# Rearranging the opening of a Fourier-mixing and MLP kernel: x ahead of the weights, exponents on GpSimd, weight conversion between the first steps

## The chip, the cores and the metric

The kernel runs on one core of one Trainium2 chip. The metric is the device time of one execution in microseconds (us), as the median of several; most times of one kernel agree within about 0.3%, and a difference counts as faster or slower only beyond 2%. The profile is one execution recorded by the hardware profiler. Its engines are PE (TensorE's matmuls), PEld (its weight loads), DVE (VectorE), ACT (ScalarE), POOL (GpSimd) and SP (SyncE, which here only issues DMAs).

## The reference, cut to what matters

```python
x:     (8, 3008, 256) float32
w_in:  (256, 2048), w_out: (2048, 256)      # reach the kernel as float64

X = np.fft.fft(np.fft.fft(x, axis=1), axis=2).real     # mixing, then 24064 tokens
h = X @ w_in
g = h * np.clip(h + 3.0, 0.0, 6.0) / 6.0               # hard swish
return g @ w_out
```

## The kernel before

The sequence transform is split as 3008 = 47 x 64. *Stage 1* transforms over 47 (after VectorE has folded x by its symmetry), the result z goes through a scratch buffer zd in DRAM, comes back as g, and *stage 2* transforms over 64 into q; a small `spread` makes the row qn. The 256-wide transform is folded into w_in. Two batches form a pair; a pair has 12 chunks of tokens, a chunk 8 steps over the hidden dimension. One step is two products u and v (`mlp1`), s, relu and gates on VectorE and ScalarE, and seven half-size block products (`mlp2`, in place of eight, paid for with sums that GpSimd makes in `combine`).

The float64 weights come as 16 pieces of 0.5 MB and are turned to float32 on the chip. Per piece:

```python
def exponent_a(j):            # ScalarE, twice: top bits to two numbers, PM
    nc.scalar.activation(low, top, AF.Identity, bias=..., scale=...)
def exponent_b(j):            # TensorE: their difference, into PSUM
    for i in range(2):
        nc.tensor.matmul(ex[:], E[:, i], PM[:, j % 2, i].bitcast(F16), ...)
def exponent_c(j):            # ScalarE: to the bits of a power of two
    nc.scalar.activation(exs[j][:].bitcast(I32), exs[j][:], AF.Identity, scale=2.0 ** 23)
def mantissa(j):              # VectorE, two operations ("top")
    ...
def join(j):                  # VectorE: mantissa times power ("wi", or blocks of G)
    ...
```

Pieces of w_in are then multiplied by the transform on TensorE (the *fold*, `wps`); pieces of w_out are mixed into seven blocks of G. The schedule is by hand: the order in which the program issues an engine's instructions is the order in which the traces show them. In the opening the pieces travel beside x; 15 of the 16 are read before the first step, and the last is finished beside the first few (its join ran at 100.18 us):

```python
for c in range(NXC):                    # 8 chunks of x
    if c + 2 < NXC:
        load_x(first, c + 2)
    load_w(c + 2)
    fold_first(first, c)                # (the last chunk: fold)
    on_scalar(c); on_vector(c)          # one step of the conversion pipeline
    ...stage 1...
    on_tensor(c)
load_g(first, 0)
for j in range(NXC, 15):                # the other pieces
    load_w(j + 2); on_scalar(j); on_vector(j); keep_awake(1); on_tensor(j)
...
for i in range(2):
    stage2(first, 0, i)
spread(first, 0)
...
for s, (p, ck, fc) in enumerate(steps): # 384 steps
    mlp1(*chunk(s + 2)); combine(*chunk(s + 1)); ...; mlp2(*chunk(s))
```

Of the kernel before, what the change touches and what calls it, by code (L numbers as in the profile page):

```python
# [51 lines left out]

PROD = ("P1", "P2", "-P4", "P5", "P7", "-P6", "P3")
# [3 lines left out]
def kernel(  # L57
# [51 lines left out]
    F = consts.tile([PR + 2, 5 * PZ + NP * NXC + 1], F32, name="F")  # L109
# [17 lines left out]
    def x_tile(pr, i):  # L127
        pool, tag = xpool, "x"
        if pr.p == 0 and 4 <= i < 13:
            pool, tag = ((apool, "a"), (cpool, "c"), (spool, "t"))[(i >= 8) + (i >= 11)]  # L130
        return pool.tile([PR + 2, XC, D], F32, tag=tag, name="xt")
# [8 lines left out]
    def load_forward(pr, c):  # L140
        xt = x_tile(pr, 2 * c)

        nr = PR + 2 if pr.p < NP - 1 else PR
        rows = x_pn[pr.p * PR:pr.p * PR + nr]
        n = XC if c < NXC - 1 else XC - 1
        nc.gpsimd.dma_start(out=xt[0:nr, 0:n, :], in_=rows[:, c * XC + 1:c * XC + 1 + n, :])
        if n < XC:
            nc.gpsimd.dma_start(out=xt[0:nr, n:XC, :], in_=rows[:, 0:1, :])
        pr.x[c] = xt

    def load_partners(pr, c):
        xr = x_tile(pr, 2 * c + 1)
# [31 lines left out]
    def fold_first(pr, c):  # L184
        xt, xr = pr.x[c][0:PR], pr.xr[c][0:PR]
        r = xr[:, ::-1, :]
        y = ypool.tile([PR, XC + 1, D], F32, tag="y", name="y")
        tt = nc.vector.tensor_tensor
        tt(y[:, 0:XC, 1:P], xt[:, :, D - 1:P:-1], r[:, :, 1:P], op=AL.add)
        tt(xt[:, :, 1:P], xt[:, :, 1:P], r[:, :, D - 1:P:-1], op=AL.add)  # L190
        tt(xt[:, :, 0:P + 1:P], xt[:, :, 0:P + 1:P], r[:, :, 0:P + 1:P], op=AL.add)
        pr.y[c] = y

    def stage1_first(pr, c, i):
        sl = slice(2 * i, 2 * i + 2)
        a, b = pr.x[c][0:PR, sl, :], pr.y[c][:, sl, 1:P]
        ps = bank([P, 2, D], "ps1")
        for k, (f, m, c0) in enumerate([(F[0:PR, 0:PZ], a[:, :, 0:P + 1], 0), (F[0:PR, 0:PZ], b, 1),
                                        (F[0:PR, 0:PZ], a[:, :, 1:P], P + 1), (FN[0:PR], b, P + 1)]):
            nc.tensor.matmul(ps[0:PZ, :, c0:c0 + m.shape[2]], f, m, start=(k == 0), stop=(k > 0),  # L200
                             skip_group_check=True)
        evict_z(pr, c, i, ps)
        if i == XC // 2 - 1:
            del pr.x[c], pr.xr[c]
# [9 lines left out]
    def stage1(pr, c, i):  # L214

        y = pr.y[c]
        ps = bank([P, 2, D], "ps1")
# [10 lines left out]
        evict_z(pr, c, i, ps)  # L228

    def evict_z(pr, c, i, ps):  # L230
        if i == 0:

            pool, tag = (gpool, "g") if pr.p == 0 and c % 3 == 2 else (zpool, "z")
            pr.z[c] = pool.tile([PZ, XC, D], F32, tag=tag, name="z")
            if c == 0:
                pr.zd = dpool.tile([2, NK1, 2, NS, D], F32, tag="zd", name="zd")
                pr.zq = dpool.tile([2, NK1, 2, NS], F32, tag="zq", name="zq")
        z = pr.z[c]
        nc.scalar.copy(z[:, 2 * i:2 * i + 2, :], ps[0:PZ])  # L239
        if i == XC // 2 - 1:  # L240
            nc.sync.dma_start(
                out=pr.zd[:].rearrange("b k c n d -> (b k c) n d")[:, c * XC:(c + 1) * XC, :],
                in_=z[:],
            )
            turn_column(pr, c, z)
            del pr.y[c], pr.z[c]
# [4 lines left out]
    def turn_column(pr, c, z):  # L251
        n = XC if c < NXC - 1 else XC - 1
        zc = zpool.tile([PZ, XC], F32, tag="zc", bufs=4, name="zc")
        nc.scalar.activation(zc[:, 0:n], z[:, 0:n, P], AF.Identity, scale=F[0:PZ, 5 * PZ + NP * NXC:])
        cs = slice(c * XC, c * XC + n)
        nc.sync.dma_start(out=pr.zq[:, :, ::-1, cs].rearrange("b k c n -> (b k) c n"), in_=zc[:, 0:n])
        if n < XC:
            nc.sync.dma_start(out=pr.zq[:, :, :, c * XC + n].rearrange("b k c -> (b k c)"), in_=z[:, n, P])


    def load_g(pr, gr):
        g = gpool.tile([P, 2 * KK, D + 1], F32, tag="g", name="g")
        ks = slice(gr * 2 * KK, (gr + 1) * 2 * KK)
        gb = [g[b * N2:(b + 1) * N2] for b in range(2)]
        for b in range(2):
            nc.sync.dma_start(out=gb[b][:, :, 0:D], in_=pr.zd[b].rearrange("k c n d -> (c n) k d")[:, ks, :])
        for b in range(2):
            nc.sync.dma_start(out=gb[b][:, :, D], in_=pr.zq[b].rearrange("k c n -> (c n) k")[:, ks])
# [36 lines left out]
    class Chunk:  # L305
# [3 lines left out]
        def __init__(self, pr, ck):  # L309
            self.pr, self.ck = pr, ck  # L310
            self.last = ck == NCK - 1
            self.final = self.last and pr.p == NP - 1
# [81 lines left out]

    def mlp2(ch, fc):
# [78 lines left out]
    FN = wpool.tile([PR + 2, PZ], F32, tag="FN", name="FN")  # L474
# [8 lines left out]
    raw, exs, fracs, w = {}, {}, {}, {}  # L483

    def load_w(j):
        kind, n, i = PIECES[j]
        st = wpool.tile([P, 2 * WB], I32, tag="st", bufs=4, name="st")
# [17 lines left out]
    def exponent_a(j):  # L505
        top = raw[j][:].bitcast(I16).rearrange("p (n four) -> p n four", four=4)[:, :, 3]
        for i in range(2):
            low = PM[:, j % 2, i].bitcast(U8).rearrange("p (n two) -> p n two", two=2)[:, :, 0]
            nc.scalar.activation(low, top, AF.Identity, bias=bias[:, i:i + 1], scale=(1 - 2 * i) / 16.0)  # L509

    def exponent_b(j):
        ex = ps_h.tile([P, WB], F32, tag="uv", name="ex")
        for i in range(2):
            nc.tensor.matmul(ex[:], E[:, i], PM[:, j % 2, i].bitcast(F16), start=(i == 0), stop=(i == 1))  # L514
        exs[j] = ex
# [4 lines left out]
    def mantissa(j):  # L520
# [3 lines left out]
        top = wpool.tile([P, WB], I32, tag="top", bufs=2, name="top")  # L524
# [5 lines left out]
    def join(j):  # L530
        kind, n, i = PIECES[j]
        frac, ex = fracs.pop(j), exs.pop(j)[:]
        if kind == "in":
            o = wpool.tile([P, WB], F32, tag="wi", bufs=4, name="wi")
            nc.vector.tensor_tensor(o[:], frac, ex, op=AL.mult)
# [3 lines left out]
        b12 = wpool.tile([P, 2, P], F32, tag="b12", bufs=2, name="b12")[:] if i == 0 else None  # L539
        for h, g in enumerate((block(n, 0), b12) if i == 0 else (block(n, 1), block(n, 6))):  # L540
            f, e = (t.rearrange("p (c q h e) -> h p c q e", c=2, h=2, e=DH)[h] for t in (frac, ex))
            nc.vector.tensor_tensor(g.rearrange("p c (q e) -> p c q e", e=DH), f, e, op=AL.mult)
        if i == 0:
            w[PIECES[j]] = b12
# [4 lines left out]
    def use_pair(j):  # L549
        kind, n, _ = PIECES[2 * j]  # L550
        if kind == "in":
            fold_w_in(n)
        else:
            mix_w_out(n)

    def mix_w_out(j):

        b12 = w.pop(("out", j, 0))
        g = [block(j, i) for i in range(7)]
        tt = nc.vector.tensor_tensor  # L560
        tt(g[3], g[0], b12, op=AL.subtract)
        tt(g[5], g[6], g[3], op=AL.add)
        tt(g[2], g[5], g[1], op=AL.subtract)
        tt(g[4], g[6], b12, op=AL.subtract)

    def fold_w_in(n):

        cs = slice(n * WB, (n + 1) * WB)
        ws = [w.pop(("in", n, i)) for i in range(2)]
        sums = []  # L570
        for blk in range(2):
            ps = bank([P, WB], "wps")
            for i in range(2):
                nc.tensor.matmul(ps[:], C[:, i, blk * P:(blk + 1) * P], ws[i], start=(i == 0), stop=(i == 1))  # L574
            sums.append(ps)

        def copy():
            for blk in range(2):
                nc.scalar.copy(W1[:, blk, cs], sums[blk][:])
            nc.sync.dma_start(out=wn[n:n + 1], in_=W1[P - 1:P, 1, cs])  # L580

        copies.append(copy)


    def load_wn(n):
        nb = WB // P
        nc.sync.dma_start(out=WN[:, n * nb:(n + 1) * nb], in_=wn[n].rearrange("(j p) -> p j", p=P))
# [263 lines left out]
```

## Time and profile before

| | before |
|---|---|
| time, median of 3 | 1980.33 us (1979.98 to 1984.44) |
| span of the profiled run, mean clock granted to TensorE | 1978.3 us, 0.996 |
| TensorE busy | 1949.1 us, 99% |
| first u; end of the eighth step's products | 80.06 us; 132.4 us |

The page of the profile gives busy times and the chain of work that ended last; windows give busy time per engine in a stretch; the order in time gives start, duration, engine, source line, operation, output and inputs, and in brackets how long the engine sat idle before and what ended that. The lines of before are in the prediction.

### The profile page before, as it was taken

The page shows a single profiled execution, that of the slowest core. Times are in us where ns is not written, and L with a number is a line of the kernel's source. Part 1 is how long each engine was busy: PE and PEld are TensorE (multiplying, and loading weights), DVE is VectorE, ACT ScalarE, POOL GpSimd, SP SyncE. Part 2 cuts the span into 40 slices and gives each one's busy share as a digit, 9 for nine tenths or more (in the row PEclk, how much of TensorE's full clock was granted, in tenths as well). Part 3 has the DMA queues.
Part 4 walks back from the last instruction along what each step waited for, and adds up shares of the span by engine and source line. Part 5 has one row for each costly group of instructions (what it writes and reads, how often), then busy time and mean ns, then how long its engine had stood idle before and what let it go on. Part 6 is the DMA issues. An engine that isn't in the chain of part 4 may idle for free.

```text
span 1978.3 us, 27746 instructions
## 1 busy us (share of the span) xinstructions
PE 1949.1 (99%) x9178; PEld 1685.4 (85%) x9178; DVE 1433.5 (72%) x2775; ACT 687.9 (35%) x1164; POOL 1414.2 (71%) x1604
## 2 busy tenths in 40 slices
PE   8899999999999999999999999999999999999998
PEld 5588888888998888888898888888889888888887
DVE  5677767776787776776777776777678777777776
ACT  6533333333333333333333333333333333333332
POOL 4277778786687787777768877778667667666765
PEclk9999999999999999999999999999999999999999
DMA  9502211111111111221111221212110101111000
GB/s 307 136 26 61 51 41 46 49 49 35 27 36 51 41 49 48 54 59 24 36 32 30 63 55 44 56 41 54 37 22 23 30 14 25 26 24 28 17 20 20
DMA packets 149701, 93.31 MB, mean 47 GB/s; under 512 B 121739, under 2 KB 135055, under 8 KB 149558
## 3 DMA queue, kind: packets, MB, share of 16 engines
q1 hardware_dynamic: 139294, 57.86, 12.2%
q0 software_dynamic: 9472, 33.49, 5.9%
q8 instruction: 72, 1.18, 0.2%
q14 instruction: 71, 0.58, 0.1%
q10 hardware_dynamic: 792, 0.20, 0.0%
HBM read 54.19 MB, written 37.33 MB: 46 GB/s over the span
## 4 chain that ended last, share of the span: by engine, by line
PE 93%; DVE 2%; ACT 1%; issue 0%; DMA 0%; SPq 0%; DVEq 0%; ACTq 0%
PE acc L403 56%; PE v L334 16%; PE u L334 16%; PE ps L284 2%; PE ps L227 2%; DVE a L379 1%; DVE s L339 1%; ACT t L376 0%; ACT PM L509 0%; DVE o L461 0%; PE wps L574 0%; DVE u L360 0%; PE ps L224 0%; PE ex L514 0%; PE awake L597 0%
## 5 line engine op out<-in xcount | busy, mean ns | idle before, releaser
L393 POOL TENSOR_TENSOR c<-a 128x512 f32<-128x512 f32 (+1 forms) x383 | 478.2, 1248 | 431.4 <-PE acc L403 369.3
L403 PE MATMUL acc<-c,G 128*128 128x256 f32 (+1 forms) x3072 | 712.0, 375 | 0.0
L376 ACT ACTIVATE t<-u,half 128x512 f32<-128x512 f32 (+1 forms) x384 | 261.0, 680 | 1100.5 <-DVE u L349 1018.7
L403 PEld LDWEIGHTS acc<-c,G 128*128 128x128 f32 x3072 | 577.5, 190 | 72.7
L339 DVE SCALAR_TENSOR_TENSOR s<-qn,WN,u 128x256 f32<-128x256 f32 (+1 forms) x768 | 330.0, 471 | 354.3 <-PE u L334 354.0
L403 PE MATMUL acc<-a,G 128*128 128x256 f32 (+1 forms) x2304 | 551.2, 375 | 0.0
L403 PEld LDWEIGHTS acc<-a,G 128*128 128x128 f32 x2304 | 433.8, 190 | 55.9
L334 PE MATMUL v<-q,W 127*128 127x256 f32 (+1 forms) x1536 | 390.1, 376 | 4.4 <-DVE a L379 4.4
L334 PE MATMUL u<-q,W 128*128 128x256 f32 (+1 forms) x1536 | 388.3, 375 | 2.4 <-DVE a L379 2.1
L379 DVE SCALAR_TENSOR_TENSOR a<-t,u 128x512 f32<-128x512 f32 (+2 forms) x448 | 263.7, 600 | 104.9 <-ACT t L376 102.1
L334 PEld LDWEIGHTS u<-q,W 128*128 128x128 f32 x1536 | 285.7, 190 | 58.2 <-issue 14.8
L334 PEld LDWEIGHTS v<-q,W 127*128 127x128 f32 x1536 | 288.7, 190 | 45.1 <-DVE a L379 4.1
L393 POOL TENSOR_TENSOR c<-c,a 128x256 f32<-128x256 f32 (+1 forms) x383 | 274.8, 717 | 30.0
L393 POOL TENSOR_TENSOR c<-a,c 128x256 f32<-128x256 f32 (+1 forms) x383 | 274.6, 717 | 30.1
L349 DVE TENSOR_TENSOR u<-s,v 128x512 f32<-128x512 f32 x352 | 245.0, 696 | 37.7 <-PE v L334 0.8
L379 DVE SCALAR_TENSOR_TENSOR a<-t,v 128x512 f32<-128x512 f32 (+1 forms) x480 | 263.2, 564 | 0.0
L376 ACT ACTIVATE t<-v,half 128x512 f32<-128x512 f32 (+1 forms) x384 | 260.5, 678 | 0.0
L351 DVE TENSOR_TENSOR v<-v,s 128x512 f32<-128x512 f32 x352 | 243.7, 692 | 0.0
L393 POOL TENSOR_TENSOR r<-w,e 128x256 f32<-128x256 f32 (+1 forms) x94 | 90.8, 987 | 3.7
L411 ACT ACTIVATE e<-acc 128x512 f32<-128x512 f32 (+2 forms) x190 | 86.3, 545 | 3.4 <-PE acc L403 3.3
L461 DVE STREAM_TRANSPOSE o<-r 128x256 f32<-128x256 f32 (+1 forms) x192 | 72.5, 414 | 0.2
L239 ACT COPY z<-ps 96x512 f32<-96x512 f32 x64 | 37.2, 582 | 83.7 <-PE ps L227 65.2
(91 smaller groups left out, 780.2 us busy)
## 6 DMA issues: line engine op xcount, KB each, us to landing
out_dram<-o SPq DMA_DIRECT2D x746, 32.0 KB
zd<-z SPq DMA_DIRECT2D x32, 384.0 KB
g<-zd SPq DMA_DIRECT2D x48, 256.0 KB
xt<-in_x_dram POOLq DMA_DIRECT2D x21, 384.0 KB, 4.1
qn<-qd SPq DMA_DIRECT2D x19, 256.0 KB
st<-in_moe_w_in_dram POOLq DMA_DIRECT2D x8, 512.0 KB, 9.1
st<-in_moe_w_out_dram POOLq DMA_DIRECT2D x8, 512.0 KB, 5.1
xt<-in_x_dram POOLq DMA_DIRECT2D x7, 376.0 KB, 3.9
```

Of the source, the lines that this page charges most:

```text
L227: nc.tensor.matmul(ps[0:PZ], F[0:PR, 0:PZ], y[:, 2 * i:2 * i + 2, :], start=True, stop=True)
L284: nc.tensor.matmul(ps[:, blk, u * P:n].rearrange("p (b k) -> p b k", b=2), g[:, kk, blk * (P + 1):blk * (P + 1) + P], T[:, :, gr, blk, kk, ...
L334: nc.tensor.matmul(ps[:, i, 0:nq], W1[r, blk, f * P:(f + 1) * P], q[r, blk, of:of + nq], start=True, stop=True)
L339: nc.vector.scalar_tensor_tensor(s[:, i, 0:nq], qn[:, of:of + nq], WN[:, f:f + 1], u[:, i, 0:nq], op0=AL.mult, op1=AL.add)
L349: nc.vector.tensor_tensor(u[:], s[:], v[:], op=AL.add)
L351: nc.vector.tensor_tensor(v[:], v[:], s[:], op=AL.subtract)
L376: nc.scalar.activation(t, h, AF.Relu, bias=half[:], scale=scale)
L379: nc.vector.scalar_tensor_tensor(dst, t, 1.0, h, op0=AL.min, op1=AL.mult)
L393: (eng or nc.gpsimd).tensor_tensor(out, in0, in1, op=AL.add)
L403: nc.tensor.matmul(ch.acc[i // 2][:, i % 2, 0:ch.n], G[:, i, fc, :], mv, start=(fc == 0 and i % 2 == 0), stop=(fc == NF - 1), skip_group_c ...
L411: nc.scalar.mul(ch.e[:, k:i + 1, 0:ch.n], ch.acc[i // 2][:, 0:i + 1 - k, 0:ch.n], 1.0 / WS)
L461: nc.vector.transpose(o[:, 0:n // DH, h], ch.r[:, m, h, 0:n].rearrange("p (j i) -> p j i", i=DH))
```

## The change

The intent: TensorE is the bound, and only in the first 132 us does it do other work than the result's. So x is loaded ahead of all weights; only the 16 of 96 scratch rows of z that the first group of tokens needs are stored at once, the others later; GpSimd subtracts the exponents in place of TensorE; the fold of w_in is made in halves of 256 columns; only pieces 0 to 5 are converted before the first step, the others between the first eight steps; and the first chunk is done by eight plain block products (as four of 512 columns), which need no mixed G. Cut to its core:

```diff
 def exponent_a(j):
     ...
-def exponent_b(j):
-    ex = ps_h.tile([P, WB], F32, tag="uv", name="ex")
-    for i in range(2):
-        nc.tensor.matmul(ex[:], E[:, i], PM[:, j % 2, i].bitcast(F16), ...)
+    nc.gpsimd.tensor_tensor(exs[j][:], *(PM[j % 2][:, i].bitcast(F16) for i in range(2)), op=AL.subtract)
 def join(j):
-            nc.vector.tensor_tensor(o[:], frac, ex, op=AL.mult)
+            (nc.vector if starting[0] else nc.gpsimd).tensor_tensor(o[:], frac, ex, op=AL.mult)
...
+                nc.sync.dma_start(out=zd[0:n0], in_=z[0:n0])       # first group
+                later.append((zd[n0:], z[n0:]))
+            pool, tag = (zpool, "z") if k < 2 else (apool, "a") if k < 6 else (qpool, "q")   # where z lies
...
+def mlp2_first(ch, fc):                       # plain products, no combine
+    for h in range(2):
+        for f in range(2):
+            nc.tensor.matmul(ch.acc[h][:], G[:, (B11, B12, B21, B22)[2 * f + h], fc, :], a[:, :, f], ...)
...
+def head(j):
+    exponent_a(j); mantissa(j)
+    if j in NEXT: load_w(NEXT[j])
+def tail(j):
+    exponent_c(j); join(j)
+    ...                                       # notes the folds that are due
...
+for c in ORDER[0:3]:
+    load_x(first, c)
+for k, c in enumerate(ORDER):
+    ...fold, stage 1, load_x of chunk k + 3; pieces only when x is through...
+load_g(first, 0)
+head(0); head(1); keep_awake(1); tail(0); keep_awake(1, w[PIECES[0]])
+head(2); tail(1); fold_w_in(*folds.pop(0)); head(3); tail(2); copy_all(); tail(3); head(4)
+for i in range(2): stage2(first, 0, i)
+spread(first, 0)
+fold_w_in(*folds.pop(1)); copy_all()
+for dst, src in later: nc.sync.dma_start(out=dst, in_=src)
...
+DUE = [(6, 7), (8, 9, 10), (11, 12), (13, 14), (15,), (), (), ()]
+mlp1(*chunk(0)); ...folds...; tail(4); head(5); tail(5)
 for s, (p, ck, fc) in enumerate(steps):
+    if s < NF:
+        for j in DUE[s][:1]: head(j)
+        copy_all()
+        mlp1(*chunk(s + 1))
+        for j in DUE[s][:1]: tail(j)
+        for j in DUE[s][1:2]: head(j)
+        mlp2_first(*chunk(s))
+        for j in DUE[s][1:2]: tail(j)
+        for j in DUE[s][2:]: head(j)
+        fold_all()
+        for j in DUE[s][2:]: tail(j)
+        ...
```

## The prediction

> **What bounds the kernel now.** I read the page from the top: busy shares, slices, the chain that ended last, then the first 140 us by tens and in order of time.
>
> ```profile
> PE 1949.1 (99%) x9178; PEld 1685.4 (85%) x9178; DVE 1433.5 (72%) x2775; ACT 687.9 (35%) x1164; POOL 1414.2 (71%) x1604
> ...
> PE 93%; DVE 2%; ACT 1%; issue 0%; DMA 0%; SPq 0%; DVEq 0%; ACTq 0%
> ```
>
> TensorE (PE) is the bound for the whole span, so nothing but its own work counts, except in the opening. There PE's busy time holds much that isn't the result: warming, waits, weight conversion. The chain, in order of time, shows where the dense part begins:
>
> ```profile
> 92.06 3.53 PE acc L403 x14
> ...
> 108.31 1.13 PE v L334 x4
> 109.44 3.02 PE acc L403 x14
> 112.46 0.86 PE u L334 x4
> 113.33 0.86 PE v L334 x4
> ...
> 129.34 3.02 PE acc L403 x14
> ```
>
> One step is u 0.86, v 0.86, seven products 3.02: 4.74 us, and there are 384 (4 pairs, 12 chunks, 8 steps). From 108 us on they are back to back. The eighth step's products end at 129.34 + 3.02 = 132.4 us, with ten steps' u and v done and both halves of the second group's stage 2. That is my marker: behind it 1846 us follow (1978.3 - 132.4), which the change hardly touches. The case is what happens to 132.4.
>
> ```profile
> 40.00:50.00 10.00, 7.02 (x29) 4.29 (x28) 7.90 (x22) 6.63 (x12) 0.74 (x2) 0.93 1.04 355
> 50.00:60.00 10.00, 9.72 (x26) 5.27 (x25) 5.95 (x10) 5.69 (x10) 2.15 (x3) 0.73 0.60 163
> 60.00:70.00 10.00, 8.86 (x23) 3.52 (x22) 4.28 (x9) 6.69 (x12) 1.42 (x2) 1.00 0.85 221
> 70.00:80.00 10.00, 8.15 (x38) 4.79 (x38) 7.69 (x19) 5.65 (x10) 0.00 (x0) 1.00 0.66 147
> ```
>
> The columns after each stretch are PE, PEld, DVE, ACT and POOL busy, clock, DMA share, GB/s. Up to 50 us the DMA engines are full (286 to 355 GB/s): x of the first pair (8 chunks of 0.77 MB, estimated from shapes) shares them with weight pieces of 0.5 MB. From 50 to 77 us it is one weight piece after another, in order:
>
> ```profile
> 69.28 1.40 ACT L509 ACTIVATE PM<-st,bias 128x512 uint8<-128x512 int16 x2
> 71.15 0.58 ACT L518 ACTIVATE ex<-ex 128x512 int32<-128x512 f32 x1 [0.46 <-PE ex L514]
> 71.64 1.40 ACT L509 ACTIVATE PM<-st,bias 128x512 uint8<-128x512 int16 x2
> 73.50 0.58 ACT L518 ACTIVATE ex<-ex 128x512 int32<-128x512 f32 x1 [0.46 <-PE ex L514]
> ```
>
> Each costs ScalarE 1.40 + 0.58 plus a wait for PE: 2.36 us. Stage 2 (77.4) and the first u (80.06) stand behind them.
>
> [...]four VectorE 128x256 ops took 0.42 us at 70 us, GpSimd idle, and 1.11, 0.83, 0.83, 1.48 at 101 us beside GpSimd adds. [...]here 717 ns against 0.42 us for 128x256, and 1248 ns against 0.69 for 128x512. [...]the trace grants 0.73 in 50 to 60 us, after gaps[...]. [...]last store issued at 55.35, load that waits for it at 57.40[...].
>
> **The change part by part.**
>
> *x first.* Three chunks are in flight; chunk k+3 is issued when chunk k is folded. Indices now arrive by a small load of their own, so the first fold starts at about 8.4 (9.11 before). A full fold on VectorE is four ops 0.61 apart and a small one, 2.6 us (first chunk 2.9, as the last one took before). Loading takes some 1.8 us of issue plus 4.5 to landing (median 5.1 for the gather, 4.1 at best): 6.2. So three chunks take 2.6 + 6.2 = 8.8, and the last fold ends near 8.4 + 2.9 + 2 x 8.8 + 2.6 = 31.5. PE needs only two products of 0.86 and a small one per chunk; stage 1 ends at 33.3 (before 53.7), the last copy of z at 33.9. The first group's stores (1/6 of the bytes) land by 37.5 beside weight loads, its g at 42.
>
> *Conversion.* GpSimd subtracts the two halves (128x512, 1.25 us) in place of two PE products. Per piece: ScalarE 1.41, GpSimd 1.25, ScalarE 0.58, join. Pieces 0 to 3 in ScalarE's order from 33.9: second weight block joined at 40.1, PE's half fold (1024 columns, 1.72) ends at 41.8. Stage 2 and spread, 2.7 us, run from 42.0; second half fold 44.7 to 46.4; copy 47.0; first u at 47.0 (80.06 before: 33 us earlier). [...]the first s is at 49.7 and gates end at 53.3.
>
> *What comes back.* Eleven pieces now lie between the first eight steps, each on the in-order queues of ScalarE and GpSimd. PE work from 47.0 to the marker: ten u and v, 17.2; eight plain block products (four of 512 columns, 2048 for 1792: 3.45 us each) 27.6; six half folds 10.3; stage 2 halves 1.8. Sum 56.9, end 103.9 with no wait. But piece 5 starts only after the first step's relu: 53.2 ScalarE, GpSimd subtraction to 57.0 (one VectorE op in between[...]), 57.6, G written by 59.5; first products end at 60.5, PE idle from 53.6. Pieces 6 and 7 follow; PE's folds of them wait until 66.8 and end at 70.2. Step 2: u, v, products to 75.4; folds of pieces 8 and 9 wait for 79.2, end 82.6. Step 3 needs piece 11's G: ends at 89.3. Then PE runs nearly free: 94.5, 99.7, 104.9, 110.1, 116.2, and 118.7 with the last u and v and the stage 2 halves. Waits thus 14.8 us of the 71.7.
>
> Gain: 132.4 - 118.7 = 13.7 us. Of the 33 us won at the first u, 14.8 go to new waits and about 5 to PE work moved behind it: folds 10.3 and plain products 3.4 more, less the 8 or so that PE lost between steps before. Time: 1980.3 - 13.7 = 1966.6; I put 1966.
>
> **The rivals.** *PE-bound opening:* conversion hides under PE. For it: ScalarE needs in steps 1 to 5 some 10 pieces x 2.0 + 6.9 of relu + 3.5 of copies = 30 us, PE 33. Against: both queues are in order and alternate through GpSimd. It would give 104 at the marker, 1952. [...]If each of 22 ops waits 0.6 us more than I placed, and half reaches PE, 6 to 7 us are lost: 1973. *The x pipeline:* if loads land in 7 to 8 us, as before under load (up to 15), stage 1 ends 3 to 5 us later: 1970. *A wait in the steady part:* the second group's spread is now at step 12, needed at 14, with 16 stores of results ahead of it in SyncE's queue at about 0.6 us each. 9.5 us of slack[...]: a few us at most. *Nothing gained:* every us won at the first u returns as waits, 1978. I doubt it; before, PE spent 27 us on conversion alone.
>
> **Range and chances.** Terms add, and each is uncertain by 3 to 6 us; hops of semaphores[...] are left out, and so is a cold clock, while overlap of issues goes the other way. 1952 to 1978. Faster by 2% is below 1940.7: it needs the marker at 92.8, below the 103.9 without any wait, hence 0.03. Slower by 2% (2020) would need damage in the steady part: 0.02.
>
> **What would show it.** Right: last stage 1 product near 33, first u near 47, first products ending near 60, PE busy under 70% between 50 and 85 us with waits put to GpSimd (wi and G), eighth products ending near 116, and the steady part equal within 2 us. Wrong: first u after 52 (x pipeline or g slower), no PE gap before the folds (PE-bound), the last G after 105, GpSimd ops of 128x512 f16 well over 1.3 us, or PE waits after step 10.

The 717 and 1248 ns are GpSimd's adds of 128x256 and 128x512 in the trace of before (`c`), the 0.42 and 0.69 us beside them VectorE's operations of these shapes.

## The result

The changed kernel took 1988.60 us (median of 4, 1986.19 to 1991.45) where the kernel before took 1980.15 in the same rounds: 8.45 us more. The ratio is 1.0038, with a 95% interval of 1.0019 to 1.0057. Ratios here are the mean time of one kernel's fast runs over that of the other's of the same rounds, so not quite the ratio of the medians. The verdict at 2% is "same", but the time is outside the predicted range.

The page of the changed kernel, busy times and the chain by engine:

```profile
PE 1942.8 (98%) x9074; PEld 1670.4 (84%) x9074; DVE 1439.6 (72%) x2754; ACT 686.5 (35%) x1162; POOL 1434.3 (72%) x1627
...
PE 92%; DVE 3%; DMA 2%; ACT 1%; issue 1%; POOL 1%; SPq 0%; DVEq 0%; ACTq 0%; POOLq 0%
```

PE does 6.3 us less work, and yet the end comes 8.7 us later (spans 1987.0 and 1978.3): it waits more. DMA, which had 0% of the chain, now has 2%. From its longest pieces in order of time (start, us, what), and its last steps before the steady part:

```profile
36.38 5.22 DMA zd<-z
...
42.41 6.75 DMA g<-zd
...
49.30 3.59 PE ps L285 x16
...
58.42 4.93 DMA zd<-z
...
75.94 5.23 PE spare L583 x14
...
91.24 6.10 PE spare L583 x14
...
102.67 4.42 PE acc L405 x6
...
131.36 3.44 PE acc L405 x8
...
138.93 1.13 PE v L336 x4
```

The store of z, the load of g, a store that the first gates wait for, and then PE groups that take 3.59, 5.23, 6.10 and 4.42 us, where the same groups at full clock, in runs told below, take 2.02, 3.29, 3.29 and 2.84. The eighth step's products end at 131.36 + 3.44 = 134.8 us (before: 132.4; predicted: 116.2). The 1.13 of v at the end follows a wait of 1.54 us for a gate, at the place where the program goes over from one step ahead to two.

The same windows as those that the prediction shows of before, and one more (columns after each stretch: PE, PEld, DVE, ACT and POOL busy, granted clock, DMA share, GB/s):

```profile
40.00:50.00 10.00, 5.48 (x13) 3.25 (x14) 7.43 (x9) 5.28 (x10) 3.86 (x4) 0.62 0.73 240
50.00:60.00 10.00, 9.76 (x51) 8.70 (x50) 3.00 (x6) 3.20 (x6) 2.12 (x2) 0.87 0.37 99
60.00:70.00 10.00, 6.41 (x22) 3.61 (x20) 6.25 (x13) 7.07 (x13) 6.40 (x8) 1.00 0.87 260
70.00:80.00 10.00, 5.26 (x14) 3.58 (x13) 4.54 (x5) 4.15 (x7) 6.35 (x7) 0.66 0.59 162
...
90.00:100.00 10.00, 8.69 (x24) 6.47 (x24) 4.93 (x6) 3.38 (x7) 4.94 (x5) 0.66 0.20 53
```

The columns to look at are PE busy and the clock. From 60 to 80 us PE is busy 11.7 of 20 us, and no other engine is full either: that is a chain of waits through all of them, not a bound. And in four of the five windows the clock is below 0.9, so that even the busy time is partly half speed (the granted clock was 0.50 from 44 to 52 us, for one). What such a chain looks like, in order of time, for pieces 8 and 9:

```profile
85.02 0.62 ACT L536 ACTIVATE ex<-ex 128x512 int32<-128x512 f32 x1
...
85.73 1.27 POOL L554 TENSOR_TENSOR wi<-top,ex 128x512 f32<-128x512 f32 x1 [8.06 <-ACT ex L536]
85.76 1.53 DVE L544 TENSOR_SCALAR top<-st 128x512 int32<-128x512 int32 x1
...
87.09 1.21 POOL L533 TENSOR_TENSOR ex<-PM 128x512 f32<-128x512 f16 x1
87.32 1.52 DVE L545 SCALAR_TENSOR_TENSOR top<-st,top 128x512 f32<-128x512 uint32 x1
...
89.14 0.74 POOL L515 DMA_DIRECT2D st<-in_moe_w_out_dram  x1 [0.85 <-DVE top L545]
...
89.91 1.28 POOL L554 TENSOR_TENSOR wi<-top,ex 128x512 f32<-128x512 f32 x1
...
91.24 6.10 PE L583 MATMUL spare<-wi,C 128*128 128x256 f32 x14 [3.49 <-POOL wi L554]
```

ScalarE's exponent of piece 8 comes only at 85.02 because it stands behind the relu of the step, which waits for PE's u and v (81.0). GpSimd had been idle for 8.06 us. Then GpSimd does join, subtraction, issue of the next load, join, one after the other; VectorE's mantissa operations, 0.42 and 0.69 us when GpSimd is idle, take 1.53 and 1.52 beside it; the issue of the load waits 0.85 us for the mantissa; and the folds on PE wait 3.49 us for the second join, and then run at half clock.

### The profile page after: what moved, and what is told of

Its sections match the earlier page's. It is cut to its first block, busy times and chain, and to the rows that moved or that the text cites. A ratio compares the mean times of both kernels' runs of the same rounds, so it can differ in the third digit from the quotient of the medians.

```text
span 1987.0 us, 27532 instructions
## 1 busy us (share of the span) xinstructions
PE 1942.8 (98%) x9074; PEld 1670.4 (84%) x9074; DVE 1439.6 (72%) x2754; ACT 686.5 (35%) x1162; POOL 1434.3 (72%) x1627
## 3 DMA queue, kind: packets, MB, share of 16 engines
q1 hardware_dynamic: 135174, 57.76, 12.4%
## 4 chain that ended last, share of the span: by engine, by line
PE 92%; DVE 3%; DMA 2%; ACT 1%; issue 1%; POOL 1%; SPq 0%; DVEq 0%; ACTq 0%; POOLq 0%
PE acc L421 55%; PE u L336 16%; PE v L336 16%; PE ps L285 2%; PE ps L213 2%; DMA xt<-in_x_dram,IX 1%; DVE a L381 1%; PE acc L405 1%; DVE s L341 1%; ACT t L378 1%; PE spare L583 1%; DMA zd<-z 1%; DVE o L479 0%; DVE u L362 0%; DMA g<-zd 0%
## 5 line engine op out<-in xcount | busy, mean ns | idle before, releaser
L395 POOL TENSOR_TENSOR c<-a 128x512 f32<-128x512 f32 (+1 forms) x375 | 467.9, 1248 | 403.1 <-PE acc L421 352.5
L421 PE MATMUL acc<-c,G 128*128 128x256 f32 (+1 forms) x3008 | 696.9, 374 | 0.0
L421 PEld LDWEIGHTS acc<-c,G 128*128 128x128 f32 x3008 | 565.4, 190 | 71.1
L421 PE MATMUL acc<-a,G 128*128 128x256 f32 (+1 forms) x2256 | 538.8, 374 | 0.0
L421 PEld LDWEIGHTS acc<-a,G 128*128 128x128 f32 x2256 | 423.4, 190 | 54.9
L395 POOL TENSOR_TENSOR c<-a,c 128x256 f32<-128x256 f32 (+1 forms) x375 | 268.6, 716 | 29.4
L395 POOL TENSOR_TENSOR c<-c,a 128x256 f32<-128x256 f32 (+1 forms) x375 | 268.3, 716 | 29.4
L213 PE MATMUL ps<-y,F 94*96 94x512 f32 x120 | 61.3, 601 | 5.2 <-ACT q L288 5.2
```

What stands on the lines that cost most here:

```text
L213: nc.tensor.matmul(ps[0:PZ], F[0:PR, 0:PZ], y[:, 2 * i:2 * i + 2, :], start=True, stop=True)
L395: (eng or nc.gpsimd).tensor_tensor(out, in0, in1, op=AL.add)
L421: nc.tensor.matmul(ch.acc[i // 2][:, i % 2, 0:ch.n], G[:, i, fc, :], mv, start=(fc == 0 and i % 2 == 0), stop=(fc == NF - 1), skip_group_c ...
```

## The experiments

Eighteen kernels ran, all with correct results. What is compared below are the ratios with their intervals, mostly about 0.2% (4 us) to either side. The table gives the difference of the medians to the kernel before in the same rounds, since its own median moved between 1980.0 and 1983.1 us from one set of rounds to another.

A caution for reading single profiles against each other: the last copy of z ends at 36.4 us in the change, and anywhere from 34.3 (e11) to 38.4 us (e15) in the other profiled executions, although these edits leave the loads of x, the folds and stage 1 as they are (e5 and e8, which add a small load there, are left out). So some us between two profiles' clock times need not come from the edit. Lengths within a profile are firmer, but they scatter too.

| run | us | before | difference | ratio and 95% interval |
|---|---|---|---|---|
| the change | 1988.60 | 1980.15 | +8.45 | 1.0038 [1.0019, 1.0057] |
| e1 awake | 1982.80 | 1983.08 | -0.28 | 1.0006 [0.9988, 1.0025] |
| e2 pieces first | 1994.76 | 1983.08 | +11.68 | 1.0069 [1.0051, 1.0088] |
| e3 joins on VectorE | 1990.14 | 1983.08 | +7.06 | 1.0038 [1.0020, 1.0055] |
| e4 order of stores | 1987.93 | 1983.08 | +4.85 | 1.0032 [1.0014, 1.0050] |
| e5 exponents on TensorE | 1996.50 | 1980.01 | +16.49 | 1.0080 [1.0063, 1.0097] |
| e6 loads late | 1983.48 | 1980.01 | +3.47 | 1.0020 [1.0003, 1.0037] |
| e7 pieces ahead, awake | 1974.83 | 1980.01 | -5.18 | 0.9970 [0.9954, 0.9987] |
| e8 pieces first, TensorE | 2001.00 | 1980.01 | +20.99 | 1.0108 [1.0092, 1.0125] |
| e9 order alone | 1976.88 | 1981.68 | -4.80 | 0.9973 [0.9943, 1.0004] |
| e10 together, awake | 1970.94 | 1981.68 | -10.74 | 0.9942 [0.9921, 0.9963] |
| e11 together, asleep | 1969.40 | 1981.68 | -12.28 | 0.9937 [0.9915, 0.9959] |
| e12 together, loads late | 1970.60 | 1981.68 | -11.08 | 0.9941 [0.9920, 0.9963] |
| e13 awake twice | 1968.56 | 1980.65 | -12.09 | 0.9934 [0.9920, 0.9947] |
| e14 order and stores | 1976.58 | 1980.65 | -4.07 | 0.9974 [0.9956, 0.9991] |
| e15 order and piece 5 | 1973.65 | 1980.65 | -7.00 | 0.9957 [0.9938, 0.9975] |
| e16 moves without order | 1981.69 | 1980.65 | +1.04 | 1.0002 [0.9984, 1.0019] |
| e17 awake twice, shorter | 1967.54 | 1980.73 | -13.19 | 0.9929 [0.9911, 0.9947] |
| e18 piece 11 earlier | 1972.34 | 1980.73 | -8.39 | 0.9947 [0.9928, 0.9965] |

### e1: TensorE kept awake

```diff
+def busy(n):                       # results thrown away
+    ps = ps_d.tile([P, 2 * TB], F32, tag="d", name="busy")
+    for i in range(n):
+        nc.tensor.matmul(ps[:], ones[:], C[:]..., start=True, stop=True)
...
     tail(0)
+    busy(4)
...                                 # and at five more places where PE waits
```

> Products that nobody reads fill the places where TensorE stood idle (4 and 5 ahead of the first half fold, 2 ahead of stage 2, 2 ahead of the second u, 5 ahead of each of the two late groups of folds, 2 ahead of the third step's products). Theory A, the halved clock: in the changed kernel's trace the granted clock was 0.50 from 44 to 52 us and 0.66 in 70 to 80 and 90 to 100, and work on the chain took longer than at full clock: stage 2 3.59 for 1.8, late folds 5.2 and 6.1 for 3.0 each, third products 4.4 for 2.6, rest of the first half fold 2.9 for 1.3; 10 us in sum. A expects 7 to 10 us off, 1979 to 1982. Rival B, the in-order queues alone: the time saved on TensorE is waited for elsewhere, 0 to 3 us off, 1986 to 1989.

With idle products in PE's waits the clock stays at 1.00 in every window of the first 150 us. The time is 8.7 us under that of the change (-0.28 against +8.45), and the eighth step's products end at 126.9 us instead of 134.8. So the halved clock costs 6 to 9 us: 8.7 by these differences, 7.9 at the eighth step's end, 6.3 by the ratios (0.0032 of 1980). One window of e1, to be held against the change's with a clock of 0.66:

```profile
70.00:80.00 10.00, 9.28 (x34) 6.18 (x33) 4.31 (x7) 3.29 (x6) 5.24 (x6) 1.00 0.49 151
```

How long the half clock lasts can be read from windows of 0.1 us. In the change it holds from 42.35 to 52.59, 73.07 to 79.90, 90.14 to 96.97 and 103.79 to 107.21: 10.24, 6.83, 6.83 and 3.41 us. The trace of before has two such stretches between 36 and 150 us, of 6.83 and 3.41 us. All six last 3.41 us or two or three times that; windows of 1 us give 13.6 and 6.8 us in e9 and 6.8 and 6.8 in e11. PE is busy in 20.05 of the change's 27.3 us of half clock; at full clock that work would take half, so these stretches lengthen PE's work by 10 us (an estimate from these figures), of which 6 to 9 reach the end.

The rounds between the steps are still long: the folds of pieces 6 and 7 end at 77.75, those of 8 and 9 at 91.13, 13.4 us apart.

### e2: all pieces before the first step

```diff
-    DUE = [(6, 7), (8, 9, 10), (11, 12), (13, 14), (15,), (), (), ()]
+    DUE = [()] * 8
-    mlp1(*chunk(0)); ...; tail(4); head(5); tail(5)
+    for j in range(5, 16):
+        head(j); tail(j - 1); copy_all(); fold_all()
+    tail(15); copy_all()
+    mlp1(*chunk(0))                # and all joins on VectorE
```

> All weight pieces are converted ahead of the first step, one head ahead of each tail, joins on VectorE; loads of x, deferred stores, plain first chunk and exponents on GpSimd stay. Theory B (pieces between the steps wait in in-order queues behind relu and the steps' own waits): 11 pieces took from 58 to 120 us between the steps, 5.6 us each; ahead of them they should take 2.5 to 3, so the first u comes near 75 to 80, the eighth products end near 118 to 122, and the time is 1966 to 1973. Rival: a piece costs the same wherever it stands (GpSimd 1.2 for the subtraction[...]): then nothing is gained, 1985 or more.

A clear miss: 11.68 us slower than before. A piece still takes 3.4 us in the mean (the joins of pieces 4 to 14 start from 57.72 to 92.12 us, 2.3 to 5.4 apart), although no step stands between: in six of ten pieces one of VectorE's two mantissa operations takes 1.5 to 2.0 us beside GpSimd's subtraction, and ScalarE, whose queue now holds the copies of the folded weights, waits 3.98 and 1.94 us for two folds, made largely at half clock (0.62 between 60 and 70 us). And in VectorE's queue the first gates stand behind all of the mantissas, as the order in time shows:

```profile
82.30 1.03 PE L336 MATMUL u<-q,W 128*128 128x256 f32 x4
96.62 2.08 PE L336 MATMUL v<-q,W 127*128 127x256 f32 x4 [13.29 <-DVE a L381]
```

The second v waits 13.29 us for PSUM that the first gates free. What follows: the conversion is long in itself when its engines hand over piece by piece, and in this arrangement it did not pay to take it out from beside the steps.

### e3: late joins on VectorE

```diff
-            (nc.vector if starting[0] else nc.gpsimd).tensor_tensor(o[:], frac, ex, op=AL.mult)
+            nc.vector.tensor_tensor(o[:], frac, ex, op=AL.mult)
-            nc.gpsimd.tensor_tensor(block(n, g)..., f, e, op=AL.mult)
+            nc.vector.tensor_tensor(block(n, g)..., f, e, op=AL.mult)
```

> Only the joins of the late pieces go from GpSimd to VectorE. Theory C[...]: VectorE's mantissa ops took 1.5 us instead of 0.42 and 0.69 beside GpSimd's joins and subtractions, and a join costs GpSimd 1.27 against 0.68; C expects 4 to 8 us off, 1981 to 1985. Rival B: the queue order is untouched and VectorE's queue has relus' and gates' waits in it too; within 2 us of the changed kernel, 1987 to 1991.

The ratio to the kernel before is the same as the change's, 1.0038. A join takes 0.69 us on VectorE against 1.27 on GpSimd, but where it is done does not matter to the end here.

### e4: the deferred stores in another order

```diff
-    for dst, src in later:
+    for dst, src in later[2:6] + later[:2] + later[6:]:
```

> The deferred stores whose source buffers the first gates reuse go first in SyncE's queue, two ahead of before. The first gate waited 3.4 us for such a store. If that wait is on the path: 2 to 3 us off, 1986. If G of piece 5 sets the first products anyway: 0, 1988 to 1989.

Four of the tiles of z lie in buffers that the first gates write to. In the change the gates wait 3.43 us for one of their stores; here the first gate runs at 59.67 without that wait. The median is 0.7 us under the change's, 3.6 by the differences to before and 1.2 by the ratios; the intervals of the two ratios overlap. That it gained is not settled by this run; e14 comes back to it.

### e5: exponents back on TensorE

```diff
-        nc.gpsimd.tensor_tensor(exs[j][:], ...subtract)
+        exs[j] = (ps_h if starting[0] else ps_d).tile([P, WB], F32, tag="uv" if starting[0] else "d", name="ex")
+        for i in range(2):
+            nc.tensor.matmul(exs[j][:], E[:, i], PM[j % 2][:, i].bitcast(F16), ...)
                                    # joins on VectorE, TensorE kept awake as in e1
```

> TensorE kept awake as in the run before, and the exponents back on TensorE (two products of 512 columns into one PSUM bank), so that the join is VectorE's[...] and GpSimd has no part in the late pieces; the places of the pieces between the steps stay. Reference is the awake run, 1982.8. Theory C'[...]: in the awake run a round of two weight pieces took 13.4 us on the chain, of which subtraction 1.2, two joins 2.5, a weight load's issue 0.75[...] are GpSimd's; without them a round should be 9 to 10, over three rounds 8 to 12 us off: 1971 to 1975. Rival B, the place in ScalarE's queue behind relu: 1.4 + 0.6 per piece and the relu's wait stay, so at most 3 us off, 1980 or more.

A miss: 16.49 us slower than before. Without GpSimd's subtractions and joins the mantissas mostly take 0.42 and 0.69 us again (of 24 between 50 and 130 us, three took 1.10 and one 0.58), so that their 1.5 us came from GpSimd's work beside them is confirmed in the main; by what mechanism is not shown. But the exponents now share PE's queue with the products and one PSUM bank with each other, and PE waits for joins to free it, up to 4.58 us at a time. The run shows what this arrangement costs; since the single bank is mine, it doesn't show what GpSimd's part alone is worth.

### e6: loads of pieces 6 to 9 later

```diff
-    NEXT = {0: 8, 1: 9, 4: 10, 5: 11, 6: 12, 7: 13, 8: 14, 9: 15}
+    NEXT = {4: (6, 7, 8, 9, 10), 5: (11,), 6: (12,), 7: (13,), 8: (14,), 9: (15,)}
                                    # TensorE kept awake as in e1
```

> Awake run with one edit: weight pieces 6 to 9 are asked for after the fourth head instead of before the first group's g. Theory D, DMA: in the changed kernel the last store of the first group took 5.2 us and g 6.8 to land, beside weight loads at 400 GB/s; without them 3 to 4 each, so g lands 4 to 5 us earlier (45 in place of 49), but stage 2 stands behind the first half fold (47): 2 us off, 1980 to 1981. Rival: g's small rows set its time by themselves, g still at 48 to 49, no gain, 1983. A loss of over 2 us would mean that pieces 6 to 9 then arrive too late.

With fewer loads on their way stage 2 starts 2.3 us earlier than in e1 (47.09 instead of 49.36) and the first u at 51.50 instead of 53.84. Of these 2.3 us, 1.4 are the last copy of z, which ended earlier in this execution (35.65 us, 37.05 in e1). But the load of g gained more than stage 2 shows, since PE still stood at its idle products: its traffic is over 3.7 us after its issue (40.71 to 44.4), in e1 6.3 (42.38 to 48.7). Then the gain is lost and more. In order of time:

```profile
60.01 0.48 DVE L341 SCALAR_TENSOR_TENSOR s<-qn,WN,u 128x256 f32<-128x256 f32 x1 [6.46 <-DMA WN<-W]
```

The second s waits 6.46 us for WN, a row of W1 that small DMAs turn into a column, and they now run beside the five loads that were put off. So does the deferred store that the first gates wait for: 8.47 us, 4.93 in the change. The run is 3.75 us slower than e1 by the differences to before. Moving the bulk loads moved the wait, from one small transfer on the path to others.

### e7: both pieces of a round ahead of the step, TensorE kept awake

```diff
-            for j in DUE[s][:1]: head(j)
+            for j in DUE[s][:2]: head(j)
+            for j in DUE[s][:2]: tail(j)
             copy_all()
             mlp1(*chunk(s + 1))
-            for j in DUE[s][:1]: tail(j)
-            for j in DUE[s][1:2]: head(j)
             mlp2_first(*chunk(s))
-            for j in DUE[s][1:2]: tail(j)
```

> Awake run (fewer idle products ahead of the late folds), with both pieces of a step's round put ahead of that step's u, v and relu on every queue, heads first, then tails. Theory B, queue order: on the chain of the awake run the conversion of pieces 8, 9 and 11 starts only when relu of the step has run, which waits for u and v behind the folds of the round before; 13.4 us a round should become 9 to 10, 6 to 10 us off in three rounds: 1973 to 1977. Rival C: the engines, not the order, set the round (GpSimd 6.5 us and VectorE[...] 5 to 6 us for two pieces), then at most 2 us: 1981 or more.

The edit also takes idle products away: three and two, in place of five and five, ahead of the two late groups of folds. 5.18 us faster than before, with an interval that excludes 1, and 4.9 us better than e1 (7.1 by the ratios; 6 to 10 were expected): both heads and both tails stand on ScalarE, VectorE and GpSimd before the relu that has to wait for PE. The folds of pieces 6/7 end at 78.8 and those of 8/9 at 89.2, 10.3 us apart instead of 13.4.

### e8: pieces first, exponents on TensorE

```diff
                                    # e2 and e5 together, one idle product per piece
```

> All pieces ahead of the first step as in the second run, but with exponents on TensorE, joins on VectorE from PSUM, TensorE kept awake. Theory C': the second run's 3.5 us a piece were [...]GpSimd (mantissa ops at 1.5, G joins at 1.3); without GpSimd 2.0 to 2.4 a piece, 16 pieces from 36 us end near 74 to 78, eighth products near 124 to 128, 1972 to 1978. Rival: ScalarE's order and the loads set it: pieces still 3 us or more each, 1985 or more.

The slowest of all, +20.99 us. Each piece still takes 3.3 us. Exponent, join and idle product form one ring through a single PSUM bank: the exponent of a piece waits for the join of the piece before (the idle product between the two waits 1.55, 1.60 and 1.44 us for joins, before 59.54, 62.88 and 66.07 us). It says of the hardware no more than e5 does, and of the plan that more engines in one ring do not shorten it.

### e9: the order alone

The edit is that of e7, on the change itself, with no idle product.

> The changed kernel with one edit: in the first eight steps both pieces of a round are read, converted and joined ahead of the step's first products, relu and gates, instead of around them; no idle products, so TensorE may still fall to half clock. Theory B (a round is 13.4 us long because the second piece's instructions stand in the queues of ScalarE, VectorE and GpSimd behind a relu and gates that wait for TensorE) expects a good part of the 8.0 us that this order gave on top of the idle products: 1979 to 1983 us where the kernel before takes 1980. Rival (the order pays only at full clock, since at half clock the folds themselves fill the rounds) expects 1985 to 1988.

The order alone takes 13.2 us off the change (-4.80 against +8.45; 12.9 by the ratios), somewhat more than its theory expected. Its interval is the widest of all and just includes 1, so it is not shown to beat the kernel before; but it lies clear of the change's. Idle products on top of it give nothing that shows (e7: -5.18). In order of time, the round of pieces 6 and 7:

```profile
69.47 0.63 ACT L536 ACTIVATE ex<-ex 128x512 int32<-128x512 f32 x1 [2.17 <-POOL ex L533]
...
71.34 0.63 ACT L536 ACTIVATE ex<-ex 128x512 int32<-128x512 f32 x1 [1.24 <-POOL ex L533]
...
72.90 2.51 POOL L554 TENSOR_TENSOR wi<-top,ex 128x512 f32<-128x512 f32 x2
...
74.23 6.89 PE L583 MATMUL spare<-wi,C 128*128 128x256 f32 x16 [3.68 <-POOL wi L554]
```

Both exponents are through before the next relu (73.48), and the two joins follow each other. The folds still wait 3.68 us and run at half clock (0.50 from 74 to 80 us), 6.89 us, but the next round's folds (86.12, 3.62 us) do not wait at all.

### e10 and e11: order and three moves in the opening

```diff
-    tail(2); copy_all(); tail(3); head(4)
+    tail(2); tail(3); copy_all(); head(4)
+    fold_w_in(*folds.pop(1))               # the fold of pieces 2 and 3
+    copy_all()                             # (e10: busy(2) after it)
     for i in range(2): stage2(first, 0, i)
     spread(first, 0)
-    fold_w_in(*folds.pop(1)); copy_all()
-    for dst, src in later:
+    for dst, src in later[2:6] + later[:2] + later[6:]:
...
+    tail(4); head(5); tail(5)              # piece 5 before the first u and v
     mlp1(*chunk(0))
     ...folds...
-    tail(4); head(5); tail(5)
```

> The best order (idle products, both pieces ahead of the step) with three more moves: the deferred stores start with the tiles whose buffers the first gates take over; piece 5 is converted before the first u and v; and the fold of pieces 2 and 3 and its copies stand before stage 2, where TensorE waits for the gather anyway. If the remaining loss before the first products lies in these waits (3.45 us of VectorE for a store, 1.48 us and more for the G of piece 5, 0.72 us for the norms' row), the first products end 5 to 8 us earlier than the 69 us of the run with the pieces ahead, and the time is 1966 to 1971 us. Rival: the converting engines are the bound of the whole stretch up to the third step, whatever waits come before; then the third step's products still end near 96 us and the time stays at 1973 to 1976 us.

> The same moves without a single idle product. If the half clock after TensorE's waits costs what it cost the changed kernel (5.9 us), it is 4 to 6 us slower than its twin with idle products: 1971 to 1976 us. Rival: with shorter waits the clock stays up by itself, and the two agree within 1.5 us.

Both land in the expected range of e10: 10.74 us (with idle products) and 12.28 us (without) faster than before. The expectation of e11 was a miss. Its rival is right about the size (1.54 us apart) but not about the reason: the clock does fall, and the idle products of e10 stand in the way as much as they help. With them PE is busy 10.00 of 10 us in every window from 50 to 110 us. In e11, without them:

```profile
57.30 3.60 PE L405 MATMUL acc<-a,G 128*128 128x512 f32 x8
63.77 7.11 PE L583 MATMUL spare<-wi,C 128*128 128x256 f32 x16 [2.87 <-POOL wi L554]
```

The first products run through without a wait and end at 60.9 (70.5 in the change); the folds wait 2.87 us, and then take 7.11 us at half clock (0.50 from 64 to 70 us).

### e12: the loads late again

The edit is that of e6, on e10.

> The twin with idle products, and the loads of pieces 6 to 9 asked for only after the fifth piece's head, so that the gather of the first group has the DMA queues to itself. In the earlier run of late loads the gather landed 2.2 us sooner but the first s waited 6.5 us for the small copies of the norms' row behind those loads; with the fold ahead of stage 2 that row is written before the loads. If contention on the gather is then worth its 2.2 us, 1964 to 1969 us, 1 to 2 us under the twin. Rival: pieces 6 to 9 then come late themselves, and it is equal or slower than the twin by up to 4 us.

-11.08 against e10's -10.74: equal within the noise. It doesn't tell what the earlier gather is worth, because PE's stage 2 stood behind the idle products before it (49.33 to 51.05 us), as in e10, while g's traffic was over by 44.5 us.

### e13 and e17: idle products at two waits only

```diff
     tail(0)
+    busy(7)                                # e17: busy(4)
...
             mlp2_first(*chunk(s))
+            if s == 0:
+                busy(6)                    # e17: busy(3)
```

> The kernel with all moves and no idle products, and idle products in two places only, where its trace shows TensorE waiting: seven before the first fold (a wait of 3.78 us) and six between the first products and the folds of pieces 6 and 7 (2.87 us, after which these folds took 7.11 us where 3.62 is their time at full clock). If those halved stretches are on the path, it gains the 3.5 us of the folds and up to 1 us before the gather: 1965 to 1967 us. Rival: the next wait (the G of piece 11, or the loads) takes the gain up, and it stays within 1.5 us of 1969.4.

> As the run awake in two places, with four idle products (3.4 us in a wait of 3.78) before the first fold and three (2.6 us in a wait of 2.87) before the folds of pieces 6 and 7. If the halved clock of these folds is on the path, it gains 2.5 to 4 us on the twin without idle products: 1965 to 1967 us where the kernel before takes 1980.5. Rival: the later waits take the gain up: 1968 to 1970 us.

e13 brought nothing (-12.09 against -12.28). One idle product is two matmuls in the trace (x6 below for three), 0.86 us, and six of them took 5.31 us in a wait of 2.87. With fewer, e17 has the lowest median, 1967.54 us, 13.19 us under before, and lies between what theory and rival expected; its interval overlaps those of e10 to e13:

```profile
61.71 2.74 PE L607 MATMUL busy<-C,ones 128*128 128x512 f32 x6
64.74 0.70 PE L583 MATMUL spare<-wi,C 128*128 128x256 f32 x2 [0.29 <-POOL wi L554]
65.97 3.29 PE L583 MATMUL spare<-wi,C 128*128 128x256 f32 x14 [0.53 <-POOL wi L554]
```

The folds take 4.0 us instead of 7.11, but start 1.0 us later and wait 0.53 us between for the second join, so that they end at 69.3 instead of 70.9. By the times about 1 us reaches the end (-13.19 against -12.28; 1.6 by the ratios), within the noise. Part of that is the start: the last copy of z ended 1.8 us later in e17's execution than in e11's. From that copy to the end of the eighth products it is 80.0 us in e11, 78.0 in e13 and 76.9 in e17, one execution of each.

### e14, e15, e16: the moves one by one

e14 is e9 with the stores of e4; e15 is e9 with piece 5 before the first u and v; e16 has the three moves of e11 and the order of the change.

> Both pieces ahead, no idle products, and only the order of the deferred stores changed. On the changed kernel that order alone gained about 1 us. If the first gates' wait of 3.4 us delays piece 5, and with it pieces 6 and 7, then with the pieces ahead it is worth 2 to 4 us: 1973 to 1975 us where the order alone took 1976.9. Rival (something else ends the same waits): within 1 us of it.

> Both pieces ahead, no idle products, and only piece 5 converted before the first u and v. VectorE and ScalarE wait there between 50 and 55 us, so the conversion is free, the first products need wait for no G, and pieces 6 and 7 follow the first gates at once: 3 to 5 us less than the order alone, 1972 to 1974 us. Rival: the first gates still wait for the store, so that only 1 to 2 us come out.

> The changed kernel with the three moves in the opening but its own order of the pieces around the steps. If order and moves add, it is 7.5 us faster than the changed kernel: 1980 to 1982 us. Rival: the moves only let the first products start earlier, and the rounds, still 13 us each, give it back in part: 1983 to 1986 us.

The order of the stores is not shown to be worth anything here (-4.07 against -4.80): the first gates run without the wait, but the first products then wait 2.48 us for G of piece 5, as its rival said. Piece 5 is worth 2.2 us by the differences and 3.2 by the ratios, where 3 to 5 were expected (its absolute range of 1972 to 1974 was met). Its rival's wait is there: the gates wait 4.39 us for a deferred store, and no G hides that now, so the order of the stores may count once piece 5 is moved; no run tests that pair alone. And the moves add to the order, as e16's theory expected: without the order they take the change from +8.45 to +1.04, 7.4 us; with it from -4.80 to -12.28, 7.5 us; the order is worth 13.2 us without them and 13.3 with them. (By the ratios: 7.1 and 7.1, 12.9 and 12.9.) So close an agreement is partly luck, with intervals of 4 us and more on each; but the profiles say the same, and where: from the last copy of z to the end of the first products it is 34.1 us (the change) and 34.8 (e9) without the moves, 26.6 (e16) and 26.6 (e11) with them; from there to the end of the eighth products 64.3 (the change) and 64.5 (e16) without the order, 54.0 (e9) and 53.4 (e11) with it.

### e18: piece 11 earlier

```diff
-    DUE = [(6, 7), (8, 9, 10), (11, 12), (13, 14), (15,), (), (), ()]
+    DUE = [(6, 7), (8, 9, 10, 11), (12, 13), (14, 15), (), (), (), ()]   # on e17
```

> The same, and piece 11 read and converted beside piece 10, a step earlier, with 12 to 15 following two to a step. If the wait for its G is one of order, the third products lose their 1.43 us and the time falls by about that, to 0.5 to 2 us under the twin. Rival: GpSimd is full in that stretch (8.5 of 10 us busy in the run without idle products), so the wait only moves to the products before, and the two agree within 0.5 us.

Neither: it is 4.8 us slower than e17. The wait for the G of piece 11 shrinks from 1.75 to 0.57 us, but with four pieces in one round ScalarE's exponents stand ahead of its copy of the folded weights, and the next u waits 1.41 us for that copy and v 1.10 us for the gates behind it; after a later wait of 2.12 us, before 94.77, v takes 1.55 us in place of 1.03, with a clock of 0.83 between 90 and 100 us. It is the mechanism of the change once more, made by my own edit.

## Why the prediction was wrong

The mechanism was right: the first u came much earlier, no engine became the bound, the gain came back as waits of PE behind in-order conversion, and the steady part was nearly untouched. The sizes of two terms were wrong, and a third and fourth were left out. By the prediction's own steps:

| step | predicted | measured |
|---|---|---|
| last copy of z | 33.9 | 36.4 |
| stores of the first group landed | 37.5 | 41.6 |
| g landed | 42 | 49.2 |
| stage 2 and spread end | 44.7 | 53.8 |
| first u | 47.0 | 55.35 |
| first products end | 60.5 | 70.5 |
| folds of 6 and 7 end | 70.2 | 81.2 |
| folds of 8 and 9 end | 82.6 | 97.3 |
| third products end | 89.3 | 107.1 |
| eighth products end | 116.2 | 134.8 |

**"First u at 47.0": 8.35 us short.** The x pipeline gave 2.5 of it, in an execution where it was neither early nor late (34.3 to 38.4 us in the others). The next step, "land by 37.5 beside weight loads, its g at 42", gave 4.7: from the last copy of z to g I had allowed 8.1 us, and it took 12.8 (5.2 for the store, 7.5 with its issue for the load), while the DMA engines moved 379 GB/s between 30 and 40 us, for pieces that nobody needed yet. e6 and e12 show most of that to be the loads of pieces 6 to 9: without them g's traffic was over 8.8 and 8.3 us after the last copy of z, with them 12.4 (the change) and 11.7 (e1). Stage 2 and spread took 4.6 us instead of 2.7, because the clock was 0.50 from 44 to 52 us: 1.9. A shorter way from spread to u gave 0.7 back.

**"Waits thus 14.8 us of the 71.7": 10 us short.** From the first u to the marker with its ten u and v and both stage 2 halves, which is 134.8 + 1.73 + 0.89 = 137.4, the change needs 82.1 us; less the 56.9 of PE work that the prediction counted (and that the trace confirms: a plain step's products took 3.44 us) these are 25 us. "And so is a cold clock", said the prediction of what it left out: e1 shows 6 to 9 us for it, before the first u and here together. That was the largest single omission, although a view of before that the prediction quotes showed 0.73. The first gates' wait of 3.43 us for a deferred store was overlooked: the change puts z into the buffers that the gates take over. Taken away, no gain clear of noise showed (e4, e14), as PE then waited for G of piece 5. That VectorE's 22 mantissa operations take longer beside GpSimd was a rival of the prediction, and the size was near it: they took 10.0 us more than at 0.42 and 0.69 each, where the rival said 22 times 0.6. How much of it reaches PE is not settled: e3, e5 and e8 each removed a part of it and put something equal or worse in its place.

**Taken as given, and the real lever: the order.** The prediction placed piece after piece behind the relu of the step and called the waits the price of the change. e9 and e16 show that 13.2 us, by the medians, are not its price but the order in which the program issues each round (the tail of the first piece and all of the second stood behind the step's u, v and relu), and 7.4 more are three such orders in the opening. With both, the same operations on the same engines end in 1969.4 us (e11). They are shown by removal, and they add; the cost of the half clock overlaps with them, since shorter waits also let the clock fall less (27.3 us of half clock in the change, 20.5 in e9, 13.7 in e11): e1 gains 8.7 us without the order, e7 against e9 0.4 with it. Put the other way, with the clock kept up the order is worth 4.9 us (e7 against e1; 7.1 by the ratios), so a part of its 13.2 is half clock that it avoids.

**Past the marker.** The wait of 1.54 us at the change from one to two steps ahead was overlooked. Beyond it 2.2 us more than before are spent (1987.0 - 137.4 - 1.5 = 1848.1 against 1978.3 - 132.4 = 1845.9). PE's idle time from 140 to 1960 us, 5.8 us against 4.9, accounts for 0.9 of it; the rest I have not traced. So 18.6 + 1.5 + 2.2 = 22.3 of the 22.6 us between 1966.0 and 1988.6 have a place.

Of its signs of a wrong prediction, two showed: the first u came after 52, and the last G after 105 (joined at 120.9). A third, PE's waits after step 10, showed at its edge, as the 1.54 us in front of the tenth v. The rival "nothing gained", "every us won at the first u returns as waits, 1978", which I doubted, came true and was passed.

## What to carry to other kernels

Where work is put between the steps of an in-order machine, write down for each engine what stands ahead of each new instruction, and put the whole feeding chain before the first instruction that has to wait for the bound engine: here that order alone was worth about 13 us, as much as the whole gain that I had predicted. Look at the granted clock after each wait of a bound engine: here each stretch of half clock cost up to 1.7 us of work for every 3.41 us (an estimate, half the stretch). Check by name which buffers a later stage takes over before deferring what reads them. Idle products that keep the clock up should be shorter than the wait that they fill: six of them took 5.31 us in a wait of 2.87 (e13), three fitted (e17), though the times of the two agree within the noise.

## What these runs show of the hardware, and what they leave open

- The granted clock. Waits of 3.49 us and 2.74 us (the change, before 75.94 and 102.67 us), 2.87 us (e11, before 63.77; and before, in front of 49.17 us) and 2.12 us (e18, before 94.77 us) went with half clock, while one of 2.12 us (the change, before 64.19 us) and one of 3.48 us (e4, before 73.62 us, where the folds took 3.29 us) did not. In the change PE was busy for 1.12 of the 3.41 us before the clock fell at 103.79, and had been back at work for 1.1 us. So the length of a wait alone did not decide it; what does is not shown. The six stretches of half clock in the traces of before and the change lasted 3.41 us or two or three times that.
- DMAs beside others. Beside loads of 0.5 MB pieces the store of z took 5.2 us and the load of g 6.75 us (the change), and a small copy into WN kept VectorE waiting for 6.46 us (e6). The load of g had its traffic over 3.7 us after its issue in e6, with those loads put off, and 6.3 us in e1. How the time grows with what runs beside it is not shown.
- The order of a queue. One engine's place in the program order became another engine's wait through two or three queues. Here that was the largest effect, 13.2 us (e9), on kernels with the same operations on the same engines.
